# Attention probabilities turned once in float32 and split into high and low parts behind the transpose

## The chip, the cores and the metric

One core of a Trainium2 chip. The metric is the device time of one execution in microseconds (us), the median of several runs. The engines are named as in the profile: PE (matmuls) with PEld (its weight loads), DVE (VectorE), ACT (ScalarE), POOL (GpSimd), SP (which issues the DMAs).

## What is computed

Attention with keys and values pooled by eight, then a gated feed-forward layer on its output:

```
k_p = k.reshape(B, H, 72, 8, D).mean(axis=3); v_p likewise       # B = H = 8, S = 576, D = 64
scores = (q @ k_p.T) / 8;  scores -= scores.max(-1)
attn = exp(scores);  attn /= attn.sum(-1) + 1e-9
x = (attn @ v_p)  as (4608 tokens, 512)
out = ((x @ w_a) * (x @ w_b)) @ w_out                            # w: 512x1536, 512x1536, 1536x512
```

The weights arrive as float64, all else is float32.

## The kernel before

Products keep nearly float32's accuracy by splitting each operand into a high part, rounded to float32r (the form in which PE multiplies here), and a low part, the rest: high x high, high x low and low x high are summed in PSUM. `low_part` (L170 and L171) makes a low part by a subtraction, source less high.

The 4608 tokens go through the feed-forward layer in 9 tiles of 512. A tile has 12 steps. A step (`ffn_in`, L552 to L554, and `ffn_out`, L573 to L575) is 36 matmuls of 128x512: 12 for psa, 12 for psb, 12 of the step before for acc. `gated` multiplies psa and psb into h on DVE (L530), ACT rounds hh (L533) and DVE subtracts hl. In a tile's last step acc is copied to y, by ACT and DVE in turns (L581), and stored.

Attention goes in 40 chunks of 128 queries, or 64 at the end of a batch (chunks 4, 5, 14, 15, 24, 25, 34 and 35). Chunks 0 to 3 make tile 0 and come before the first step; chunks 4 to 8 make tile 1 and are processed in tile 0's steps, which is also where the weights are converted from float64 (L211 to L226, 36 blocks: ACT two instructions each, DVE three at L213, L216 and L222, POOL one at L226) and split (`split_weight`, L238 on ACT and L171 on POOL). Chunks 9 to 39 are processed in the steps of the later tiles.

What a chunk does, in `chunk`: load and split the queries (qh, ql); scores in PSUM (psc: L392 for chunks 0 to 8, L406 and L409 for the others, four of them, each reduced from PSUM by DVE at L412 before the maximum is taken off at L376 and L377); exponential on ACT (L426); the sums z and their reciprocal on DVE (L430); the scores times z, in place (L432, POOL, or DVE for chunks 1 and 3); then the split in SBUF: pr, high parts by ACT (L441) and low parts by POOL (L171) of the first 64 keys, and rem, the eight keys that remain, laid out as high, low, high (L443 twice on ACT, L171 on POOL). Then the transposes (L477, `turn`): four for pr's high parts, four for its low parts, two for rem, each group into a PSUM tile ptr, copied out by ACT (L478) to p0, p1 and p2 (one tile "work" holds p0 and p1 in later tiles). When a block of two or three chunks is turned, its products with the values go to PSUM po (L510 to L513) and out to xh (ACT, L521) and xl (DVE, L171). psc, ptr and the later po share two PSUM banks (tag "att").

The order of the work is written out by generators. `Chains` counts slots; a step of the inner loop has six, one ahead of each six of its matmuls. In a slot the chains that are due go on, and then one chain that had yielded `PE` may place its matmuls ahead of the next six:

```
for x in range(3):
    if x < 2 or t < 2:
        yield PE
    turn(x)
    if x != 1 or t < 2:
        yield 1
mark("turned", i)
```

So in the later tiles the second and the third `turn` share one such place, and the chunk's next one comes a slot later. Keys and values of the next batches (`load_keys`, `load_values`) are loaded and summed by DVE in the same way (L258, L310).

Of the kernel before, what the change touches and what calls it, by code (L numbers as in the profile page):

```python
# [27 lines left out]
# the high word of float64 2**-126, read as float32  # L28
# [38 lines left out]
# the same before the first step: chunks one after the other, the values, the second batch's keys,  # L67
# the weights' loads and how much later their conversion begins
# [3 lines left out]
class Chains:  # L72
    """Chains of work (generators), resumed slot by slot: a chain yields how many slots its next part
    comes later, or PE to get TensorE between two groups of the inner loop's products. done holds
    what has been issued."""
# [6 lines left out]
    def mark(self, *what):  # L82
        self.done.add(what)
# [30 lines left out]
def attn_moe_kernel(ctx: ExitStack, tc: tile.TileContext, q, k, v, vr, wa, wb, wo, out):  # L114
# [12 lines left out]
    ident0 = tmp("ident0")[:, :P]  # L127
    make_identity(nc, ident0)
    ident = const.tile([P, P], F32R, name="ident")
    raw = {name: const.tile([P, NF, 512], F32, name=f"w{name}_raw") for name in ("a", "b", "o")}  # L130
    w_dram = {"a": wa, "b": wb, "o": wo}
    # pooled keys, heads in pairs on the diagonal: [(h%2, d), h//2, hi/lo, h%2, key]
    kdiag = [const.tile([P, NK, 2, 2, SP], F32R, name=f"kdiag{i}") for i in range(2)]
    # pooled values, heads in pairs on the diagonal: [(h%2, key), h//2, hi/lo, (h%2, d)]
    vdiag = [const.tile([P, NK, 2, P], F32R, name=f"vdiag{i}") for i in range(2)]
    # row (part, h%4, key) belongs to which of four heads
    mask = const.tile([P, 4], F32, name="mask")
    # where the weights' bits arrive: later the place of the blocks' transposed probabilities
# [6 lines left out]
    # chunks of a batch and a tile whose products with the values are made together  # L145
    blocks, start = [], 0

    def cut(chunks, limit):
        """the cheapest blocks: a product takes its columns' time, or that of its weights' load"""
        best = None  # L150
        for x in range(1, len(chunks) + 1):
            total = sum(flat[c][2] for c in chunks[:x])
            if total > limit:
                break
            cost, rest = cut(chunks[x:], limit) if x < len(chunks) else (0, [])
            cost += max(total, 2 * P)
            if best is None or cost < best[0]:
                best = cost, [chunks[:x]] + rest
        return best
# [13 lines left out]
    # the first batch's inputs wait where the last weights come later  # L173
# [21 lines left out]
    def convert_weights(name, j, first):  # L195
        """float64 bits to the nearest float32: the sign and the exponent's top bit stay, 27 bits of
        the high word move up by three, what lies below float32's normal range becomes zero, and
        the low word rounds into the last three bits"""
# [6 lines left out]
        for f in range(NF):  # L205
# [23 lines left out]
            # not far ahead of the products, and not all three matrices at once  # L229
# [54 lines left out]
    def load_values(b):  # L284
# [31 lines left out]
        # each row's values at its head's place, zero at the others'  # L316
# [31 lines left out]
    def chunk(i):  # L348
# [18 lines left out]
        # scores less their maximum  # L367
# [32 lines left out]
        else:  # L400
# [23 lines left out]
        # probabilities  # L424
# [12 lines left out]
        yield from wait(("turned", i - 2))  # L437
# [9 lines left out]
        mark("probs", i)  # L447
        yield PROBS_GAP

        # transposed, and a block's products with the values  # L450
# [4 lines left out]
        if i == members[0]:  # L455
            turned[j] = {}

        def turn(x):
            rows = P if x < 2 else NR
            num = NK if x < 2 else NG  # L460
            if x not in turned[j]:
                if tile_of[i] < 2:
                    turned[j][x] = sb.tile([P, num, BLOCK], F32R, tag=f"p{x}", name=f"p{x}_{j}", bufs=1)
                elif x == 0:
                    both = sb.tile([P, 2, NK, BLOCK_LATER], F32R, tag="work", name=f"p_{j}", bufs=1)
                    turned[j].update({0: both[:, 0], 1: both[:, 1]})
                else:
                    turned[j][x] = sb.tile([P, NK * BLOCK], F32R, tag="p0", name=f"p{x}_{j}", bufs=1)[
                        :, :NG * BLOCK_LATER
                    ].rearrange("p (g s) -> p g s", g=NG)  # L470
            dst = turned[j][x]
            pt = ps.tile([P, 512], F32, tag="att", name=f"ptr_{i}_{x}", bufs=2)
            ptr = pt.bitcast(F32R).rearrange("p (g s) -> p g s", g=NK)
            for g in range(num):
                src = pr[:n, x, 2 * g:2 * g + 2, :] if x < 2 else rem[:n, g]
                src = src.rearrange("p a s -> p (a s)") if x < 2 else src.rearrange("p a c s -> p (a c s)")
# [3 lines left out]
        yield from wait(("turned", i - 1), ("value", j - 1))  # L480
# [17 lines left out]
        th, tl, tr = (turned[j][x] for x in range(3))  # L498
# [85 lines left out]
    def have(t):  # L584
        """all chunks of a tile are done"""
        return all(("value", block_of[i]) in done for i in range(len(flat)) if tile_of[i] == t)

    with tc.manual_schedule():
        load_early()
        nc.vector.tensor_copy(ident, ident0)  # L590
        for t in kdiag + vdiag:
            nc.gpsimd.memset(t.bitcast(F32), 0.0)
        nc.vector.tensor_reduce(
            out=mask[:NR], in_=ident0[:NR, :NR].rearrange("p (a c s) -> p c a s", a=3, c=4), axis=AX.XY, op=ALU.add
# [91 lines left out]
```

## Time and profile before

| | us |
|---|---|
| median of 3 runs | 1107.91 (1107.82 to 1108.48) |
| span of the profiled execution | 1107.4 |
| PE busy | 1038.7 (94%) |
| DVE busy | 611.5 (55%) |
| ACT busy | 522.9 (47%) |
| POOL busy | 618.8 (56%) |

The span is what the profile shows from the first to the last instruction; the time of a run, as it is measured, holds a little more. The profile gives the busy shares of the span as a whole, and the stretches of it differ: the first 215 us hold the attention of the first two tiles, the weights' conversion and tile 0's steps. PE is busy without a break after them. A matmul's duration in the trace is longer than the distance from its start to the next one's, since matmuls overlap in the array; its cost in a full queue is that distance.

### The profile page before, as it was taken

How to read it: one execution, taken by the hardware profiler on the slowest of the kernel's cores; microseconds unless marked ns; L12 is line 12 of the kernel's file. 1: busy time of each engine (PE TensorE's matmuls, PEld its weight loads, DVE VectorE, ACT ScalarE, POOL GpSimd, SP SyncE). 2: the span in 40 equal slices, each digit the busy share in tenths (PEclk: the TensorE clock that was granted, in tenths of full speed). 3: DMA queues.
4: the chain of work that ended last, by engine and by line, in shares of the span. 5: the costliest groups of instructions: out<-in, count | busy, mean ns of one | idle time of the engine just before them, and what ended most of it. 6: DMA issues, size and time to landing. Idle time of an engine off the chain costs nothing.

```text
span 1107.4 us, 13650 instructions
## 1 busy us (share of the span) xinstructions
PE 1038.7 (94%) x4964; PEld 861.7 (78%) x4964; DVE 611.5 (55%) x917; ACT 522.9 (47%) x1051; POOL 618.8 (56%) x501
## 2 busy tenths in 40 slices
PE   4378887899999999999999999999999999999998
PEld 4356665688887888888888888888888888888887
DVE  7999999863348333753367335654458343332212
ACT  3655555544445445544455445444445444443332
POOL 6557776655555555555555455554556455554442
PEclk9989888999999999999999999999999999999999
DMA  6454344120023000400021002200211020001001
GB/s 220 128 154 126 105 145 131 48 89 1 1 71 110 1 1 22 148 3 1 1 94 59 1 1 91 82 1 1 69 55 49 1 67 1 1 1 38 1 1 38
DMA packets 29874, 59.59 MB, mean 54 GB/s; under 512 B 7120, under 2 KB 7120, under 8 KB 29808
## 3 DMA queue, kind: packets, MB, share of 16 engines
q1 hardware_dynamic: 29808, 58.73, 16.9%
q8 instruction: 39, 0.64, 0.3%
q14 instruction: 27, 0.22, 0.1%
HBM read 49.28 MB, written 9.44 MB: 53 GB/s over the span
## 4 chain that ended last, share of the span: by engine, by line
PE 81%; DVE 14%; issue 2%; DMA 1%; ACT 1%; POOL 0%; SPq 0%; DVEq 0%; POOLq 0%; ACTq 0%
PE acc L573 9%; PE psa L552 8%; PE psb L552 8%; PE acc L575 8%; PE acc L574 8%; PE psa L554 8%; PE psa L553 8%; PE psb L554 8%; PE psb L553 8%; PE ptr L477 2%; PE psc L406 2%; DVE wo_raw L216 1%; DVE wo_raw L213 1%; DVE wa_raw L222 1%; DVE wb_raw L216 1%
## 5 line engine op out<-in xcount | busy, mean ns | idle before, releaser
L171 POOL TENSOR_TENSOR jlb<-wb_raw,jhb 128x512 fp32r<-128x512 f32 x108 | 142.9, 1323 | 220.9 <-ACT jhb L238 220.9
L530 DVE TENSOR_TENSOR h<-psb,h 128x512 f32<-128x512 f32 x108 | 74.5, 690 | 343.6 <-PE psb L554 340.4
L171 POOL TENSOR_TENSOR jla<-wa_raw,jha 128x512 fp32r<-128x512 f32 x108 | 143.9, 1332 | 143.0 <-ACT jha L238 117.5
L557 ACT COPY h<-psa 128x512 f32<-128x512 f32 x108 | 63.5, 588 | 244.1 <-PE psa L554 235.4
L573 PE MATMUL acc<-jho,hh 128*128 128x512 f32 x432 | 175.5, 406 | 0.0
L552 PE MATMUL psb<-xh,jhb 128*128 128x512 f32 x432 | 172.4, 399 | 2.1 <-DVE h L530 2.1
L552 PE MATMUL psa<-xh,jha 128*128 128x512 f32 x432 | 173.7, 402 | 0.0
L554 PE MATMUL psb<-xh,jlb 128*128 128x512 f32 x432 | 170.0, 393 | 2.4 <-POOL jlb L171 2.4
L553 PE MATMUL psa<-xl,jha 128*128 128x512 f32 x432 | 170.0, 393 | 1.0 <-DVE xl L171 1.0
L554 PE MATMUL psa<-xh,jla 128*128 128x512 f32 x432 | 170.0, 394 | 0.0
L575 PE MATMUL acc<-jho,hl 128*128 128x512 f32 x432 | 170.0, 393 | 0.0
L574 PE MATMUL acc<-jlo,hh 128*128 128x512 f32 x432 | 169.9, 393 | 0.0
L553 PE MATMUL psb<-xl,jhb 128*128 128x512 f32 x432 | 169.6, 393 | 0.0
L171 POOL TENSOR_TENSOR jlo<-wo_raw,jho 128x512 fp32r<-128x512 f32 x108 | 155.1, 1437 | 5.6 <-ACT jho L238 5.6
L171 DVE TENSOR_TENSOR hl<-h,hh 128x512 fp32r<-128x512 f32 x108 | 95.1, 880 | 20.7 <-ACT hh L533 20.6
L533 ACT CAST hh<-h 128x512 fp32r<-128x512 f32 x108 | 67.1, 622 | 72.6 <-DVE h L530 72.6
L554 PEld LDWEIGHTS psb<-xh,jlb 128*128 128x128 f32 x432 | 82.0, 190 | 20.8 <-POOL jlb L171 3.3
L575 PEld LDWEIGHTS acc<-jho,hl 128*128 128x128 f32 x432 | 81.9, 190 | 18.2 <-DVE hl L171 0.3
L554 PEld LDWEIGHTS psa<-xh,jla 128*128 128x128 f32 x432 | 82.1, 190 | 17.8
L552 PEld LDWEIGHTS psb<-xh,jhb 128*128 128x128 f32 x432 | 81.9, 190 | 17.8 <-issue 2.5
L553 PEld LDWEIGHTS psa<-xl,jha 128*128 128x128 f32 x432 | 82.4, 191 | 16.6 <-DVE xl L171 1.5
L552 PEld LDWEIGHTS psa<-xh,jha 128*128 128x128 f32 x432 | 82.2, 190 | 15.3
(92 smaller groups left out, 1776.3 us busy)
## 6 DMA issues: line engine op xcount, KB each, us to landing
out<-y SPq DMA_DIRECT2D x36, 256.0 KB, 2.2
kraw<-in_k SPq DMA_DIRECT2D x28, 288.0 KB, 3.9
vraw<-in_v SPq DMA_DIRECT2D x28, 256.0 KB, 3.1
qraw<-in_q SPq DMA_DIRECT2D x28, 256.0 KB, 3.8
words<-in_wa SPq DMA_DIRECT2D x12, 512.0 KB, 3.7
words<-in_wb SPq DMA_DIRECT2D x12, 512.0 KB, 3.7
words<-in_wo SPq DMA_DIRECT2D x12, 512.0 KB, 3.6
vraw<-in_vr SPq DMA_DIRECT2D x14, 192.0 KB, 2.6
```

The source lines that it names most:

```text
L171: eng.tensor_tensor(out=lo, in0=src, in1=hi.bitcast(F32), op=ALU.subtract)
L216: nc.vector.scalar_tensor_tensor(out=wi, in0=hi, scalar=-(1 << 30), in1=wi, op0=ALU.bitwise_and, op1=ALU.bitwise_or)
L406: nc.tensor.matmul(pt[:n, :2 * hk], qh[:, g, :n], kd[:, g].rearrange("p w e s -> p (w e s)"), start=True, stop=False)
L530: nc.vector.tensor_tensor(out=h, in0=pt, in1=h, op=ALU.mult)
L533: nc.scalar.copy(hh, h)
L552: nc.tensor.matmul(pt, wh[:, c], xh[:, kk], start=(kk == 0), stop=False)
L553: nc.tensor.matmul(pt, wh[:, c], xl[:, kk], start=False, stop=False)
L554: nc.tensor.matmul(pt, wl[:, c], xh[:, kk], start=False, stop=(kk == NK - 1))
L557: nc.scalar.copy(h, pt)
L573: nc.tensor.matmul(acc[c], hh[:, cs], wh, start=(f == 0), stop=False)
L574: nc.tensor.matmul(acc[c], hh[:, cs], wl, start=False, stop=False)
L575: nc.tensor.matmul(acc[c], hl[:, cs], wh, start=False, stop=(f == NF - 1))
```

## The change

The probabilities are not split in SBUF. Multiplied by 1/z they go into pr (128x512) and three times into rem, in float32 (POOL, four instructions; DVE for chunks 1 and 3). They are transposed once in float32: four transposes for pr, two for rem, against an identity that is float32 too. ACT rounds the high part on its way out of PSUM, and one slot later DVE subtracts it from the PSUM tile to get the low part (for rem on 32 of its 96 rows). The PSUM bank is so held until that subtraction. The wait for the transposes of the chunk two before stands ahead of the multiplication, one `yield 1` is gone, and the second turn needs no place of its own in the later tiles.

```diff
-    ident0 = tmp("ident0")[:, :P]
-    make_identity(nc, ident0)
-    ident = const.tile([P, P], F32R, name="ident")
+    ident = const.tile([P, P], F32, name="ident")
+    make_identity(nc, ident)
...
-        (nc.vector if first and i % 2 else nc.gpsimd).tensor_tensor(
-            out=s[:n], in0=s[:n], in1=z[:n].unsqueeze(2).broadcast_to([n, H, SP]), op=ALU.mult
-        )
-        yield 1
         yield from wait(("turned", i - 2))
-        pr = sb.tile([P, 2, H, KM], F32R, tag="pr", name=f"pr_{i}")
-        rem = sb.tile([P, NG, 3, 4, KR], F32R, tag="rem", name=f"rem_{i}")
-        sr = s[:n, :, KM:].rearrange("p (r c) s -> p r c s", r=NG)
-        nc.scalar.copy(pr[:n, 0], s[:n, :, :KM])
-        for x in (0, 2):
-            nc.scalar.copy(rem[:n, :, x], sr)
-        yield 1
-        low_part(nc.gpsimd, pr[:n, 1], s[:n, :, :KM], pr[:n, 0])
-        low_part(nc.gpsimd, rem[:n, :, 1], sr, rem[:n, :, 0])
+        pr = sb.tile([P, H, KM], F32, tag="pr", name=f"pr_{i}")
+        rem = sb.tile([P, NG, 3, 4, KR], F32, tag="rem", name=f"rem_{i}")
+        zb = z[:n].unsqueeze(2)
+        eng = nc.vector if first and i % 2 else nc.gpsimd
+        eng.tensor_tensor(out=pr[:n], in0=s[:n, :, :KM], in1=zb.broadcast_to([n, H, KM]), op=ALU.mult)
+        for x in range(3):
+            eng.tensor_tensor(
+                out=rem[:n, :, x],
+                in0=s[:n, :, KM:].rearrange("p (r c) s -> p r c s", r=NG),
+                in1=zb.broadcast_to([n, H, KR]).rearrange("p (r c) s -> p r c s", r=NG),
+                op=ALU.mult,
+            )
         mark("probs", i)
+        yield 1
         yield PROBS_GAP
...
         def turn(x):
...
-            ptr = pt.bitcast(F32R).rearrange("p (g s) -> p g s", g=NK)
-            for g in range(num):
...
-                nc.tensor.transpose(ptr[:rows, g, :n], src, ident[:n, :n])
-            nc.scalar.copy(dst[:rows, :, c0:c0 + n], ptr[:rows, :num, :n])
+            ptr = pt.rearrange("p (g s) -> p g s", g=NK)
+            if x == 0:
+                for g in range(NK):
+                    src = pr[:n, 2 * g:2 * g + 2, :].rearrange("p a s -> p (a s)")
+                    nc.tensor.transpose(ptr[:, g, :n], src, ident[:n, :n])
+                nc.scalar.copy(th[:, :, cs], ptr[:, :, :n])
+                yield 1
+                low_part(nc.vector, tl[:, :, cs], ptr[:, :, :n], th[:, :, cs])
+            else:
+                for r in range(NG):
+                    src = rem[:n, r].rearrange("p a c s -> p (a c s)")
+                    nc.tensor.transpose(ptr[:NR, r, :n], src, ident[:n, :n])
+                nc.scalar.copy(tr[:NR, :, cs], ptr[:NR, :NG, :n])
+                yield 1
+                lo = slice(4 * KR, 2 * 4 * KR)
+                low_part(nc.vector, tr[lo, :, cs], ptr[lo, :NG, :n], tr[lo, :, cs])
...
-        for x in range(3):
-            if x < 2 or t < 2:
+        for x in range(2):
+            if x == 0 or t < 2:
                 yield PE
-            turn(x)
-            if x != 1 or t < 2:
-                yield 1
+            yield from turn(x)
         mark("turned", i)
```

How the order of the instructions moves, at three places. First PE at the end of chunk 23 and the start of chunk 24, a chunk of 64 queries, in tile 4 (ptr_23_0, ptr_23_1: the turns of chunk 23; psc_24: scores of chunk 24; the last number of a name only counts tiles). Before:

```order
L477 MATMUL ptr_23_1_5320<-ident_69,pr_23_5250 128x128 x4
L477 MATMUL ptr_23_2_5326<-ident_69,rem_23_5251 96x128 x2
L573 MATMUL acc_4_2_5134<-jho_50_5212,hh_50_5206 128x512
L574 MATMUL acc_4_2_5134<-jlo_50_5213,hh_50_5206 128x512
L575 MATMUL acc_4_2_5134<-jho_50_5212,hl_50_5207 128x512
L573 MATMUL acc_4_3_5138<-jho_50_5212,hh_50_5206 128x512
L574 MATMUL acc_4_3_5138<-jlo_50_5213,hh_50_5206 128x512
L575 MATMUL acc_4_3_5138<-jho_50_5212,hl_50_5207 128x512
L406 MATMUL psc_24_0_5343<-kdiag0_73,qh_24_5255 64x288
L409 MATMUL psc_24_0_5343<-kdiag0_73,ql_24_5256 64x144
L406 MATMUL psc_24_1_5347<-kdiag0_73,qh_24_5255 64x288
L409 MATMUL psc_24_1_5347<-kdiag0_73,ql_24_5256 64x144
```

And in the changed kernel:

```order
L476 MATMUL ptr_23_0_5141<-ident_64,pr_23_5100 128x128 x4
L561 MATMUL psb_4_3_5128<-xh_4_4221,jhb_51_5069 128x512
L562 MATMUL psb_4_3_5128<-xl_4_4222,jhb_51_5069 128x512
L563 MATMUL psb_4_3_5128<-xh_4_4221,jlb_51_5070 128x512
L561 MATMUL psb_4_3_5128<-xh_4_4221,jhb_51_5069 128x512
L562 MATMUL psb_4_3_5128<-xl_4_4222,jhb_51_5069 128x512
L563 MATMUL psb_4_3_5128<-xh_4_4221,jlb_51_5070 128x512
L483 MATMUL ptr_23_1_5163<-ident_64,rem_23_5101 96x128 x2
L405 MATMUL psc_24_0_5170<-kdiag0_72,qh_24_5115 64x288
L408 MATMUL psc_24_0_5170<-kdiag0_72,ql_24_5116 64x144
L405 MATMUL psc_24_1_5174<-kdiag0_72,qh_24_5115 64x288
L408 MATMUL psc_24_1_5174<-kdiag0_72,ql_24_5116 64x144
```

The six products of acc between the last transposes of chunk 23 and the first scores of chunk 24 are gone from there; the scores follow at once, behind the end of psb_4_3. Then DVE's queue at the same place. Before:

```order
L530 TENSOR_TENSOR h_51_5266<-psb_4_3_5268,h_51_5266 128x512
L310 TENSOR_REDUCE vp_5_5145<-vraw_5_4_5273 96x64
L310 TENSOR_REDUCE vp_5_5145<-vraw_5_5_5274 96x64
L171 TENSOR_TENSOR hl_51_5290<-h_51_5266,hh_51_5289 128x512
L319 SCALAR_TENSOR_TENSOR vwide_5_5340<-vp_5_5145,mask_77 96x256 x2
L412 TENSOR_REDUCE s_24_5298<-psc_24_0_5343 64x144
L412 TENSOR_REDUCE s_24_5298<-psc_24_1_5347 64x144
```

And in the changed kernel (p_11 and p2_11 are the turned low parts of chunk 23):

```order
L539 TENSOR_TENSOR h_51_5126<-psb_4_3_5128,h_51_5126 128x512
L170 TENSOR_TENSOR p_11_4867<-ptr_23_0_5141,p_11_4867 128x4x128
L411 TENSOR_REDUCE s_24_5167<-psc_24_0_5170 64x144
L411 TENSOR_REDUCE s_24_5167<-psc_24_1_5174 64x144
L170 TENSOR_TENSOR p2_11_4868<-ptr_23_1_5163,p2_11_4868 32x2x128
```

The low part that frees ptr_23_0's bank stands behind h_51, and the one that frees ptr_23_1's behind both score reductions. Second, DVE at the end of tile 1's attention (xl_1 from po_4: its last block; vp_2: the sums of batch 2's values; h_10, ql_9: the step's product and chunk 9's queries). Before:

```order
L530 TENSOR_TENSOR h_10_1720<-psb_0_10_1722,h_10_1720 128x512
L310 TENSOR_REDUCE vp_2_1635<-vraw_2_2_1710 128x64
L310 TENSOR_REDUCE vp_2_1635<-vraw_2_3_1711 128x64
L171 TENSOR_TENSOR ql_9_1746<-qraw_9_1677,qh_9_1745 128x512
L171 TENSOR_TENSOR hl_10_1737<-h_10_1720,hh_10_1736 128x512
L171 TENSOR_TENSOR xl_1_933<-po_4_0_1764,xh_1_932 128x2x256
L171 TENSOR_TENSOR xl_1_933<-po_4_2_1783,xh_1_932 128x2x256
```

And in the changed kernel:

```order
L170 TENSOR_TENSOR xl_1_875<-po_4_0_1645,xh_1_874 128x2x256
L170 TENSOR_TENSOR xl_1_875<-po_4_2_1669,xh_1_874 128x2x256
L539 TENSOR_TENSOR h_10_1685<-psb_0_10_1687,h_10_1685 128x512
L309 TENSOR_REDUCE vp_2_1595<-vraw_2_2_1665 128x64
L309 TENSOR_REDUCE vp_2_1595<-vraw_2_3_1666 128x64
L170 TENSOR_TENSOR ql_9_1712<-qraw_9_1631,qh_9_1711 128x512
L170 TENSOR_TENSOR hl_10_1703<-h_10_1685,hh_10_1702 128x512
```

The two xl have moved ahead of h_10 and the vp pair. Third, ACT before the first step (ptr_2, ptr_3: the turns of chunks 2 and 3; po_1: their products with the values; wlow, wmag: the words of a weight block). Before:

```order
L478 COPY p2_1_438<-ptr_2_2_439 96x2x128
L478 COPY p0_1_407<-ptr_3_0_448 128x4x128
L211 ACTIVATE wlow_o1_454<-words_78 128x512
L212 ACTIVATE wmag_o1_455<-words_78 128x512
L478 COPY p1_1_419<-ptr_3_1_462 128x4x128
L478 COPY p2_1_438<-ptr_3_2_469 96x2x128
L521 CAST xh_0_344<-po_1_0_480 128x2x256
L521 CAST xh_0_344<-po_1_2_491 128x2x256
```

And in the changed kernel:

```order
L484 CAST p2_1_352<-ptr_3_1_411 96x2x128
L237 CAST jhb_0_415<-wb_raw_70 128x512
L210 ACTIVATE wlow_b1_422<-words_77 128x512
L211 ACTIVATE wmag_b1_423<-words_77 128x512
L530 CAST xh_0_318<-po_1_0_433 128x2x256
L530 CAST xh_0_318<-po_1_2_449 128x2x256
L210 ACTIVATE wlow_o1_460<-words_77 128x512
L211 ACTIVATE wmag_o1_461<-words_77 128x512
```

The copies of chunk 3's turns and xh of its block stand ahead of the second part of wo, no longer behind it.

## Rows read from the trace of the kernel before

**Rows 1.** Stretches: length; busy us (count) of PE, PEld, DVE, ACT, POOL; granted clock; DMA share.

```profile
25.00:66.00 41.00, 20.50 (x97) 17.44 (x98) 39.14 (x59) 24.85 (x53) 20.20 (x17) 1.00 0.48 143
66.00:215.00 149.00, 117.29 (x517) 92.39 (x515) 142.75 (x168) 79.91 (x160) 108.66 (x77) 0.86 0.39 118
215.00:1107.00 892.00, 887.98 (x4296) 739.96 (x4296) 410.10 (x660) 408.81 (x820) 473.00 (x381) 1.00 0.11 34
```

**Rows 2.** Timelines of DVE and POOL near 60 and 97 us: start, duration, instruction.

```profile
59.72 0.69 DVE L216 SCALAR_TENSOR_TENSOR wa_raw<-words,wa_raw 128x512 int32<-128x512 int32 x1
...
97.56 1.65 DVE L216 SCALAR_TENSOR_TENSOR wo_raw<-words,wo_raw 128x512 int32<-128x512 int32 x1
...
97.19 1.47 POOL L171 TENSOR_TENSOR jlb<-wb_raw,jhb 128x512 fp32r<-128x512 f32 x1
```

**Rows 3.** Groups by shape, 66 to 215 us: count | busy us, mean ns | idle before.

```profile
L216 DVE SCALAR_TENSOR_TENSOR wo_raw<-words,wo_raw 128x512 int32<-128x512 int32 x10 | 16.5, 1655 | 0.3
...
L530 DVE TENSOR_TENSOR h<-psb,h 128x512 f32<-128x512 f32 x11 | 7.5, 680 | 0.0
```

**Rows 4.** Timeline of PE, turns of a full chunk.

```profile
509.02 0.39 PE L575 MATMUL acc<-jho,hl 128*128 128x512 f32 x1
509.25 0.46 PE L477 MATMUL ptr<-ident,pr 128*128 128x128 f32 x4
509.54 0.30 PE L477 MATMUL ptr<-ident,rem 128*96 128x128 f32 x2
509.68 0.47 PE L573 MATMUL acc<-jho,hh 128*128 128x512 f32 x1
```

**Rows 5.** Timeline of PE, turns of a chunk of 64 queries.

```profile
373.90 0.50 PE L477 MATMUL ptr<-ident,pr 64*128 64x64 f32 x4
374.23 0.30 PE L477 MATMUL ptr<-ident,rem 64*96 64x64 f32 x2
```

**Rows 6.** Timelines of PE and DVE where chunk 23 is turned.

```profile
423.56 0.40 PE L554 MATMUL psb<-xh,jlb 128*128 128x512 f32 x1
...
424.07 0.69 DVE L530 TENSOR_TENSOR h<-psb,h 128x512 f32<-128x512 f32 x1 [5.82 <-PE psb L554]
```

**Rows 7.** Groups by shape, the whole span.

```profile
L171 POOL TENSOR_TENSOR pr<-s,pr 128x512 fp32r<-128x512 f32 x32 | 42.6, 1331 | 4.3 <-ACT pr L441 4.2
L432 POOL TENSOR_TENSOR s<-s,z 128x576 f32<-128x576 f32 x30 | 41.7, 1389 | 54.1 <-DVE z L430 34.9 <-ACT jha L238 19.2
...
L171 POOL TENSOR_TENSOR rem<-s,rem 128x64 fp32r<-128x64 f32 x32 | 12.7, 397 | 0.0
L581 DVE COPY y<-acc 128x512 f32<-128x512 f32 x18 | 12.4, 691 | 16.9 <-PE acc L575 16.9
...
L171 DVE TENSOR_TENSOR xl<-po,xh 128x512 fp32r<-128x512 f32 x18 | 12.2, 688 | 10.1 <-ACT xh L521 10.1
...
L412 DVE TENSOR_REDUCE s<-psc 64x144 f32<-64x288 f32 x24 | 9.7, 443 | 2.9 <-PE psc L409 2.6
...
L171 DVE TENSOR_TENSOR xl<-po,xh 128x256 fp32r<-128x256 f32 x2 | 0.8, 418 | 2.7 <-ACT xh L521 2.7
```

**Rows 8.** Waits, 25 to 66 us: total, times, longest.

```profile
PE po L510 <- ACT p L478: 6.0, 1, 6.0
```

**Rows 9.** Timelines of PE and DVE around 213 us; [idle before <- its releaser].

```profile
215.47 0.40 PE L406 MATMUL psc<-kdiag,qh 128*128 128x288 f32 x1 [2.44 <-DVE xl L171]
...
211.23 1.32 DVE L310 TENSOR_REDUCE vp<-vraw 128x64 f32<-128x512 f32 x2 [2.38 <-DMA vraw<-in_v]
...
214.74 1.27 DVE L171 TENSOR_TENSOR xl<-po,xh 128x512 fp32r<-128x512 f32 x2
```

**Rows 10.** Short stretches around two gaps of PE, columns as in rows 1.

```profile
105.70:109.10 3.40, 1.61 (x11) 1.14 (x9) 3.33 (x6) 0.00 (x0) 1.32 (x2) 1.00 0.87 245
109.10:112.50 3.40, 3.40 (x12) 2.82 (x11) 3.33 (x6) 2.68 (x5) 3.40 (x3) 0.50 0.34 134
...
214.90:218.30 3.40, 2.70 (x15) 2.28 (x16) 3.30 (x7) 0.31 (x1) 0.00 (x0) 1.00 0.00 0
```

More of the change, by code (lines that the diff above doesn't have):

```diff
@@ L431, in chunk @@
         yield 1
-        (nc.vector if first and i % 2 else nc.gpsimd).tensor_tensor(
-            out=s[:n], in0=s[:n], in1=z[:n].unsqueeze(2).broadcast_to([n, H, SP]), op=ALU.mult
-        )
-        yield 1
-        yield from wait(("turned", i - 2))
-        pr = sb.tile([P, 2, H, KM], F32R, tag="pr", name=f"pr_{i}")
-        rem = sb.tile([P, NG, 3, 4, KR], F32R, tag="rem", name=f"rem_{i}")
-        sr = s[:n, :, KM:].rearrange("p (r c) s -> p r c s", r=NG)
-        nc.scalar.copy(pr[:n, 0], s[:n, :, :KM])
-        for x in (0, 2):
-            nc.scalar.copy(rem[:n, :, x], sr)
-        yield 1
-        low_part(nc.gpsimd, pr[:n, 1], s[:n, :, :KM], pr[:n, 0])
-        low_part(nc.gpsimd, rem[:n, :, 1], sr, rem[:n, :, 0])
-        mark("probs", i)
+        yield from wait(("turned", i - 2))
+        pr = sb.tile([P, H, KM], F32, tag="pr", name=f"pr_{i}")
[10 more added lines that the diff above has]
+            )
+        mark("probs", i)
+        yield 1
         yield PROBS_GAP
@@ L454, in chunk @@
         total = sum(flat[c][2] for c in members)
-        if i == members[0]:
[L456 to L472, printed above, removed]
-            ptr = pt.bitcast(F32R).rearrange("p (g s) -> p g s", g=NK)
-            for g in range(num):
-                src = pr[:n, x, 2 * g:2 * g + 2, :] if x < 2 else rem[:n, g]
-                src = src.rearrange("p a s -> p (a s)") if x < 2 else src.rearrange("p a c s -> p (a c s)")
-                nc.tensor.transpose(ptr[:rows, g, :n], src, ident[:n, :n])
-            nc.scalar.copy(dst[:rows, :, c0:c0 + n], ptr[:rows, :num, :n])
@@ L480, in chunk, with blocks_turned @@
-        yield from wait(("turned", i - 1), ("value", j - 1))
-        for x in range(3):
-            if x < 2 or t < 2:
+        def blocks_turned():
+            if tile_of[i] < 2:
+                both = [sb.tile([P, NK, BLOCK], F32R, tag=f"p{x}", name=f"p{x}_{j}", bufs=1) for x in range(2)]
+                rem = sb.tile([P, NG, BLOCK], F32R, tag="p2", name=f"p2_{j}", bufs=1)
+            else:
+                both = sb.tile([P, 2, NK, BLOCK_LATER], F32R, tag="work", name=f"p_{j}", bufs=1)
+                both = [both[:, 0], both[:, 1]]
+                rem = sb.tile([P, NK * BLOCK], F32R, tag="p0", name=f"p2_{j}", bufs=1)[
+                    :, :NG * BLOCK_LATER
+                ].rearrange("p (g s) -> p g s", g=NG)
+            return (*both, rem)
@@ new lines, in turn @@
+        def turn(x):
+            th, tl, tr = turned[j]
+            cs = slice(c0, c0 + n)
+            pt = ps.tile([P, 512], F32, tag="att", name=f"ptr_{i}_{x}", bufs=2)
+            ptr = pt.rearrange("p (g s) -> p g s", g=NK)
[6 more added lines that the diff above has]
+                low_part(nc.vector, tl[:, :, cs], ptr[:, :, :n], th[:, :, cs])
+            else:
+                for r in range(NG):
[5 more added lines that the diff above has]
+                low_part(nc.vector, tr[lo, :, cs], ptr[lo, :NG, :n], tr[lo, :, cs])
@@ L483, in chunk @@
+        yield from wait(("turned", i - 1), ("value", j - 1))
+        if i == members[0]:
+            turned[j] = blocks_turned()
+        for x in range(2):
+            if x == 0 or t < 2:
                 yield PE
-            turn(x)
-            if x != 1 or t < 2:
-                yield 1
+            yield from turn(x)
         mark("turned", i)
@@ L497, in chunk @@
         per = min(NK, 512 // total)
-        th, tl, tr = (turned[j][x] for x in range(3))
+        th, tl, tr = turned[j]
         for g0 in range(0, NK, per):
@@ L589, in attn_moe_kernel @@
         load_early()
-        nc.vector.tensor_copy(ident, ident0)
         for t in kdiag + vdiag:
@@ L593, in attn_moe_kernel @@
         nc.vector.tensor_reduce(
-            out=mask[:NR], in_=ident0[:NR, :NR].rearrange("p (a c s) -> p c a s", a=3, c=4), axis=AX.XY, op=ALU.add
+            out=mask[:NR], in_=ident[:NR, :NR].rearrange("p (a c s) -> p c a s", a=3, c=4), axis=AX.XY, op=ALU.add
         )
```

## The prediction

> **What bounds the kernel now.** I read the busy time of the engines by stretch first [rows 1]. It falls into three parts. From 215 us to the end the matmul engine is busy 887.98 of 892 us and no other engine more than half of the time: there the length of its own queue is the time, and any gap in it is lost. From 66 to 215 us VectorE is busy 142.75 of 149 us and the matmul engine 117.29, at a mean granted clock of 0.86; from 25 to 66 us VectorE is busy 39.14 of 41 and the matmul engine half of the time. So in the first 215 us VectorE sets the pace, but not by its own work alone. One instruction of the weights' conversion, L216, takes 0.69 us when no GpSimd instruction runs when it starts, and 1.65 us when it starts 0.4 us into one [rows 2]. The ten of wo_raw average 1655 ns, while the products h of L530, which read PSUM, average 680 ns there [rows 3]. I read this as an instruction with SBUF inputs waiting for the GpSimd instruction beside it, one with a PSUM input not. The Trainium skill, "SBUF — State Buffer", puts an exclusive lock behind it: VectorE with two SBUF inputs and a GpSimd instruction that reads SBUF share a port pair. The trace agrees by the 1.65 against 0.69 us.
>
> So three prices are needed: matmul time after 215 us, VectorE time weighed against GpSimd time before it, and any new gap.
>
> **The change, part by part.**
>
> *Fewer transposes.* A chunk of 128 queries turned high, low and remainder: four, four and two transposes. The second four go. In the matmul engine's timeline the second four start at 509.25 and the remainder at 509.54; the product before them started one ordinary pitch, 0.23, earlier [rows 4]. So four cost 0.29 us. In a chunk of 64 queries it is 373.90 to 374.23, 0.33 us [rows 5]. After tile 1's chunks 31 are left, 25 full and six of 64 queries: 25 x 0.29 + 6 x 0.33 = **-9.2 us**, all of it in the stretch where the matmul queue is the time. The transposes that stay now read float32 instead of float32r. No row shows a float32 transpose; I take the same duration, as the array moves as many columns either way, and price the other case as a rival.
>
> *Six new gaps.* The second turn no longer asks for a group of the matmul engine, so in six places (chunks 14, 15, 24, 25, 34, 35, the order shows it at 24) the next chunk's scores stand straight behind the remainder's transposes, where six products stood between. The scores need a PSUM bank, and both were taken by the two turns. Formerly ScalarE's copy freed a bank; now VectorE's low part does, one slot later. At 24 this low part stands behind h in VectorE's queue, and h waits for the last product of psb. In the trace of before that last product starts at 423.56 and h at 424.07, 0.69 long [rows 6]. The low part is a 128 x 512 subtraction out of PSUM; that price is 688 ns [rows 7], so it ends at 424.07 + 0.69 + 0.69 = 425.45. The matmul engine would reach the scores at 423.56 + 0.23 + 0.14 (remainder pair, 509.54 to 509.68 [rows 4]) = 423.93: a wait of 1.5 us. The second score tile of that slot takes the bank that the first leaves, so it waits for the first's reduction: 443 ns [rows 7], plus the 0.17 by which a product outlasts its pitch (0.40 less 0.23), plus twice the 0.11 from the end of psb (423.96) to h (424.07): 0.8 us. For 14, 24 and 34 this is 2.3 each. For 15, 25 and 35 h is long done and the low part too, so 0.8 each. At 14 a copy y of 691 ns [rows 7] stands in the same queue: 0.7. Sum 6.9 + 2.4 + 0.7 = **+10.0 us**. Bounds: 0 if VectorE keeps ahead after all, and 10.0 plus the clock (below).
>
> *GpSimd and VectorE from 66 to 215 us*, chunks 4 to 8. GpSimd gave a full chunk 1389 + 1331 + 397 ns (product, low part, remainder's low part [rows 7]) = 3.12 us. Now it multiplies 512 of the 576 columns, 1389 x 512/576 = 1235, and three remainders, each at the 397 of the same size: 2.43. Five chunks: -3.5 us. VectorE gains two low parts, 688 + 418 ns by the nearest rows [rows 7]: 1.11 for the three full chunks, and for the two of half the columns 0.42, the price of 256 columns, and some 0.29 for 128: 0.71; together +4.7. If the two engines' work adds up on the shared side, -3.5 stays. What VectorE takes out of PSUM runs beside GpSimd while GpSimd has work, 108.66 of 149 us or 73% [rows 1]: 3.4 of the 4.7 us are so covered. -3.5 + 4.7 - 3.4 = **-2.2 us**. Bounds: -3.5 (all covered) to +4.7 (GpSimd's relief worth nothing, no cover).
>
> *The first 66 us*, chunks 0 to 3. VectorE gains four times 1.11 = 4.4 us, and for chunks 1 and 3, which it multiplies itself, three small products more each: at about half of GpSimd's 397 ns, as 688 stands to 1331 [rows 7], 6 x 0.2 = 1.2. GpSimd loses four low parts (4 x 1.73 = 6.9) and gains on chunks 0 and 2 (2 x (2.43 - 1.39) = 2.1): -4.8. On ScalarE the second block's copies of probabilities no longer stand behind the conversion of wo's second part, as the order shows; in the trace a product with the values waited 6.0 us for such a copy [rows 8]. Work added to the busy engine, work and waits taken from the others: I take **0**, bounds -6.0 to +5.6. ScalarE's own loss of work counts for nothing, since it is busy half of the time.
>
> *The gap at 213 us.* The scores of chunk 9 wait 2.44 us for the two xl of the last block of tile 1, which start at 214.74 because the vp reductions ahead of them waited 2.38 us for values to land [rows 9]. In the changed order xl stands ahead of that h and of the second vp pair. I take the gap as closed but for the time of ql behind the same vp: **-2.2 us**; bounds -2.4 and 0.
>
> *Nothing else costs.* The wait for ("turned", i - 2) moves ahead of the multiplication, so GpSimd's queue could hold behind it; but a chunk's turn is issued a slot sooner and there are two chunks between. The cast of the identity, one small instruction at the start, is gone. No DMA is added, and SP's queue only moves with the slots.
>
> **Sum:** -9.2 + 10.0 - 2.2 + 0 - 2.2 = -3.6. The profiled span is 1107.4 and the median of the runs 1107.91, 0.5 above it, which I put on again: 1107.9 - 3.6 = **1104.3 us**. About 0.2%, 2.2 us, is what a measurement can tell from no change.
>
> **The rivals.**
>
> *Slower: VectorE itself is the bound of the first 215 us.* If its busy share of 95 and 96% [rows 1] were its own need, GpSimd's relief would bring nothing and every added instruction would land: +4.7 in place of -2.2, +5.6 in place of 0. Then -9.2 + 10.0 + 4.7 + 5.6 - 2.2 = +8.9: 1116.8. It decides from the point where less than about 6.7 of the 10.3 added us are covered or made good. For it speaks how full VectorE is; against it the mean of 1655 ns for L216 against 0.69 alone [rows 2, 3]. 13%.
>
> *The clock falls at the new gaps.* A gap in the 3.4 us from 105.70 (matmul busy 1.61 of them) was followed by a granted clock of 0.50, 1.2 GHz, for the next 3.4 us; the 2.44 gap at 213 was followed by 1.00, 2.4 GHz [rows 9, 10]. At half the clock 3.4 us of matmul time hold 1.7 us of work. The three larger gaps could add 3 x 1.7 = 5.1: 1109.4. The matmul engine is full up to each of them, as it was at 213, which speaks against. 10%.
>
> *Float32 transposes run in four passes.* Then each transpose would take three more times its columns' time: 512 columns take 0.23, so 128 take 0.057 and a transpose gains 0.17; 25 x 6 x 0.17 + 36 x 0.085 = +28.6, giving 1132.9. The Trainium skill, "FP8 and Floating Point Precision", TensorE Precision Notes, has "True FP32: 4 passes through PE array", and by that rule this change would lose; "TensorE: Matmul & The Clock Gate", Terms, calls transpose mode 4x faster for FP32, which would undo it. No run here shows either yet. Against it speaks that the instruction is a transpose in both programs and only moves data. 7%.
>
> *Faster: the new gaps do not appear.* If VectorE has the low part done when the scores come (h a little sooner, a bank more), the +10.0 goes: 1107.9 - 13.6 = 1094.3. The order of the queue speaks against it. 8%.
>
> **How the numbers follow.** The forecast has the remaining 62%; its own range is 1099 to 1110 from the bounds of its terms taken together: faster 0.38, same 0.20, slower 0.04. The clock gives same 0.05, slower 0.05; VectorE and the four passes slower 0.13 and 0.07; no gaps faster 0.08. Together faster 0.46, same 0.25, slower 0.29. The range 1096 to 1118 takes in VectorE as the bound; it leaves out the four passes, the missing gaps and some 3% of the forecast's own tails, 18%.
>
> **What would show it.** Right: after 215 us the matmul engine has six gaps, three of about 2.3 us and three of 0.8, released by a low part or a score reduction on VectorE; 31 groups of four transposes less, and the four that stay still about 0.29 us; no gap of 2.4 at chunk 9; the steady stretch begins about 4 us sooner. Wrong: transposes whose pitch has grown; a granted clock under 1.00 after the gaps; a VectorE share of the first 215 us still at 95% and that stretch longer; or L216 unchanged in its mean though GpSimd does less, which would sink the reading of the shared side.

## The result and the profile after

The changed kernel takes 1113.06 us (median), the kernel before 1107.87 in the same comparison: ratio 1.0042, 95% interval 1.0031 to 1.0053. It is slower by about 5 us where -3.6 was forecast; a second comparison gave 1112.93, ratio 1.0037 (1.0024 to 1.0049). One of the six executions took 3590.4 us at a granted clock of 0.29; it counts in the median, which is 1112.9 without it, and not in the ratio. The time lies in the range, but on the other side of no change.

The busy times of the whole span, from the page:

```profile
span 1110.4 us, 13284 instructions
...
PE 1034.4 (93%) x4804; PEld 853.6 (77%) x4804; DVE 648.2 (58%) x1002; ACT 473.3 (43%) x891; POOL 593.8 (53%) x535
```

PE, ACT and POOL work less than before, DVE 36.7 us more, as the edit says. The stretches, columns as in [rows 1]:

```profile
25.00:66.00 41.00, 22.37 (x82) 17.84 (x83) 38.87 (x64) 22.12 (x42) 15.64 (x14) 0.75 0.44 133
66.00:215.00 149.00, 117.61 (x512) 93.24 (x511) 144.39 (x187) 73.64 (x140) 102.81 (x82) 0.87 0.39 120
215.00:1107.00 892.00, 881.26 (x4160) 730.64 (x4159) 446.29 (x717) 369.85 (x696) 459.75 (x412) 1.00 0.10 33
```

After 215 us PE is now idle for 10.7 of 892 us, where it had been idle for 4.0 [rows 1]. Of the 4.0 us, 3.4 lie behind the last matmul of the kernel before (it ends at 1103.57), of the 10.7 only 0.4 (1106.59): inside the queue it is 10.3 against 0.6. The waits of PE from 200 us on say for what (total us, times, longest; the third line is chunk 9's, at 212.75):

```profile
PE psc L405 <- DVE p L170: 6.6, 5, 1.6
PE psc L405 <- DVE s L411: 3.7, 6, 0.6
PE psc L408 <- DVE ql L170: 1.2, 1, 1.2
```

The first two are the forecast's gaps: score tiles that wait for a bank, until a low part (p) or a score reduction (s) on DVE has freed it. At chunk 24, PE in the kernel before, where six products of acc (not shown) stand between the turn of chunk 23 and the scores, and no score tile waits:

```profile
588.67 0.39 PE L554 MATMUL psb<-xh,jlb 128*128 128x512 f32 x1
...
590.95 0.30 PE L477 MATMUL ptr<-ident,rem 128*96 128x128 f32 x2
...
592.54 0.29 PE L406 MATMUL psc<-kdiag,qh 128*64 128x288 f32 x1
```

([rows 6], which the forecast took for this place, stand in tile 2, 165 us earlier. Here h starts at 589.17, 0.50 behind the last product of psb; there it was 0.51, so nothing in the forecast hangs on it.) PE and DVE in the changed kernel:

```profile
588.67 0.39 PE L563 MATMUL psb<-xh,jlb 128*128 128x512 f32 x1
588.90 0.38 PE L483 MATMUL ptr<-ident,rem 128*96 128x128 f32 x2
590.60 0.32 PE L405 MATMUL psc<-kdiag,qh 128*64 128x288 f32 x1 [1.32 <-DVE p L170]
590.76 0.23 PE L408 MATMUL psc<-kdiag,ql 128*64 128x144 f32 x1
591.60 0.35 PE L405 MATMUL psc<-kdiag,qh 128*64 128x288 f32 x1 [0.61 <-DVE s L411]
```

```profile
589.17 0.69 DVE L539 TENSOR_TENSOR h<-psb,h 128x512 f32<-128x512 f32 x1 [3.43 <-PE psb L563]
589.77 0.68 DVE L170 TENSOR_TENSOR p<-ptr,p 128x512 fp32r<-128x512 f32 x1
591.09 0.45 DVE L411 TENSOR_REDUCE s<-psc 64x144 f32<-64x288 f32 x1 [0.64 <-PE psc L408]
```

The chain is read from the stamps: the last product of psb, h, then the low part behind h to 590.45, then the scores; the reduction to 591.54, then the second score tile. Measured from start to start, less what the same pairs take without a wait, the eleven gaps sum to 12.0 us (the waits view counts only from the end of the matmul ahead, 10.3).

The two traces' first product of each step gives the account of the span. At the first step of tile 1 the changed kernel is 3.2 us ahead (220.55 against 223.77), in the end 3.0 behind. The first step of all begins 4.2 us earlier (52.96 against 57.14); 1.0 of that is lost again before tile 1.

### The profile page after: what moved, and what is told of

It reads as the page before. It is cut to its first block, busy times and chain, and to the rows that moved or that the text cites. A ratio compares the mean times of both kernels' runs of the same rounds, so it can differ in the third digit from the quotient of the medians.

```text
span 1110.4 us, 13284 instructions
## 1 busy us (share of the span) xinstructions
PE 1034.4 (93%) x4804; PEld 853.6 (77%) x4804; DVE 648.2 (58%) x1002; ACT 473.3 (43%) x891; POOL 593.8 (53%) x535
## 4 chain that ended last, share of the span: by engine, by line
PE 77%; DVE 19%; issue 1%; DMA 1%; POOL 1%; ACT 0%; SPq 0%; DVEq 0%; POOLq 0%; ACTq 0%
PE psb L561 8%; PE acc L582 8%; PE psb L563 8%; PE acc L584 8%; PE acc L583 8%; PE psb L562 8%; PE psa L561 8%; PE psa L563 7%; PE psa L562 7%; PE psc L405 2%; DVE wo_raw L215 2%; DVE hl L170 1%; DVE wa_raw L215 1%; PE ptr L476 1%; DVE wo_raw L212 1%
## 5 line engine op out<-in xcount | busy, mean ns | idle before, releaser
L170 POOL TENSOR_TENSOR jla<-wa_raw,jha 128x512 fp32r<-128x512 f32 x108 | 153.0, 1417 | 64.9 <-ACT jha L237 62.7
L170 POOL TENSOR_TENSOR jlo<-wo_raw,jho 128x512 fp32r<-128x512 f32 x108 | 157.9, 1462 | 5.6 <-ACT jho L237 5.6
L170 DVE TENSOR_TENSOR hl<-h,hh 128x512 fp32r<-128x512 f32 x108 | 105.8, 979 | 9.3 <-ACT hh L542 8.5
L582 PEld LDWEIGHTS acc<-jho,hh 128*128 128x128 f32 x432 | 82.3, 191 | 15.7
```

Source lines behind the costliest of these rows:

```text
L170: eng.tensor_tensor(out=lo, in0=src, in1=hi.bitcast(F32), op=ALU.subtract)
L582: nc.tensor.matmul(acc[c], hh[:, cs], wh, start=(f == 0), stop=False)
```

## The experiments

All were compared with the kernel before on the same chip, in five rounds or more; its median was 1107.87 to 1108.35 in these comparisons. "Changed" is 1113.06 us.

**Giving the turn its place back where 64 queries follow.**

```diff
-            if x == 0 or t < 2:
+            if x == 0 or t < 2 or (i + 1 < len(flat) and flat[i + 1][2] < P):
```

> The second turn asks for a place of its own again where the next chunk has 64 queries (chunks 13, 14, 23, 24, 33, 34), and nowhere else. Theory (the six gaps are the loss): in the trace of the changed kernel the gaps after 215 us sum to 12.0 us, and one of them is followed by 3.4 us at a granted clock of 0.50, worth 1.7. Left over should be about 1.2 at chunk 14, where a second low part still stands behind the copy y, and some 0.3 each at three places: about 11.5 us less than the changed kernel, 1101 to 1102.5 us, faster than the kernel before. Rival (the gaps only take up time in which the matmul engine would have waited later): within 2 us of the changed kernel, 1111 to 1115. Rival on the clock (the fall to 0.50 comes without the gaps too): 1103 to 1104, with such a stretch still in the steady part.

1101.87 us (1101.48 to 1102.97), ratio 0.9947 (0.9935 to 0.9960): 11.2 less than changed, and faster than before. Of the steady waits one is left, in chunk 14:

```profile
215.00:1107.00 892.00, 881.35 (x4163) 730.45 (x4162) 449.03 (x717) 370.11 (x696) 456.83 (x412) 1.00 0.11 34
```

```profile
PE psc L405 <- DVE p L170: 0.9, 1, 0.9
```

PE's busy time there is what it was with the gaps (881.35 against 881.26), but the last matmul now ends at 1097.33 instead of 1106.59, so that the idle time of this window lies behind it. No stretch from 218 us to the end is at 0.50. The six places are the loss: given back, they turn 5 us slower into 6 us faster than the kernel before.

**Only the three in front of chunks 14, 24 and 34** (the same condition with `n == P and`).

> The second turn asks for a place of its own only in chunks 13, 23 and 33, so only the gaps in front of chunks 14, 24 and 34 close (1.49 + 0.78 us each, and the 1.2 us inside chunk 14 may stay); those at 15 (1.7 + 0.78), 25 and 35 (0.78 each) stay. Theory (each gap costs its length, and the clock falls only behind the long ones): 6.8 us of gap gone, and of the stretches at 0.50 only one at chunk 15 can remain: 6 to 9 us less than the changed kernel, 1104 to 1107. Rival (short gaps bring the clock down as well): stretches at 0.50 behind 25 and 35, 1107 or more.

1104.12 us (1103.37 to 1106.15), 8.9 less than changed. The waits that are left:

```profile
PE psc L405 <- DVE s L411: 1.8, 3, 0.6
PE psc L405 <- DVE p L170: 0.9, 1, 0.9
```

The three are the score reductions at 15, 25 and 35. The low part is the one in chunk 14 that is left with six places too, so the 1.59 us in front of chunk 15 have gone as well, which was not expected. The trace shows how: chunk 14's first turn stands six products later than in the changed kernel (353.70 instead of 351.83), and its low part ends at 355.92, just ahead of the scores at 355.97. By their lengths the closed gaps are thus 6.8 + 1.7 = 8.5 of the 8.9 us, and against six places the run is 2.25 slower, where three gaps of 0.78 make 2.3: each gap costs its length. No stretch behind 219 us stood at 0.50 in this profile.

**Every second turn with a place** (`yield PE` in both passes, `x == 0 or t < 2` gone).

> Every second turn asks for a place of its own, as in the kernel before, not only the six. The matmul engine's work is the same, only spread over more slots. Theory (only the six gaps counted, sharing the place earns nothing by itself): as with six places, 1101 to 1103 us. Rival (the shared place also brings work forward that the end needs): 2 us or more slower than with six places.

1102.07 us (1100.93 to 1103.98), as with six. Sharing the place of the others neither costs nor earns anything that shows.

**The changed kernel once more.**

> The changed kernel once more, unchanged, for a second profile. The gaps should stand at the same places with the same lengths, 12 us together; what may differ is how many of the long ones are followed by a granted clock of 0.50, 0 to 4 of them, 1.4 to 1.7 us each, which would account for most of the spread of its runs (1111.5 to 1113.5).

1112.93 us (1110.55 to 1114.05). The waits are again 6.6 and 3.7 us, in the same five and six places; two of the long gaps were followed by a clock of 0.50, in the first profile it was one. Chunk 9's wait of 1.2 is not there this time. First profile, the gap at chunk 34 and what followed it, then two stretches of the second one (columns as in [rows 1]):

```profile
840.30:843.70 3.40, 1.60 (x9) 0.92 (x7) 1.66 (x3) 3.14 (x8) 2.49 (x2) 1.00 0.20 68
843.70:847.10 3.40, 3.26 (x9) 2.56 (x10) 2.22 (x5) 0.45 (x1) 1.29 (x1) 0.50 0.02 5
```

```profile
356.70:360.10 3.40, 3.40 (x12) 2.70 (x11) 1.47 (x5) 1.44 (x3) 0.26 (x1) 0.50 0.00 0
592.20:595.60 3.40, 3.40 (x10) 2.68 (x11) 2.14 (x4) 0.29 (x1) 1.29 (x1) 0.50 0.00 0
```

PE is busy there, at 1.2 GHz instead of 2.4, so each such stretch costs up to 1.7 us. In the profiles of the changed kernel and of its variants with the gaps they came behind chunks 14, 15, 24 and 34, never behind the single waits of 0.6 at 25 and 35, and not in every run.

**The kernel before with float32 transposes.**

```diff
-            ptr = pt.bitcast(F32R).rearrange("p (g s) -> p g s", g=NK)
+            ptr = pt.rearrange("p (g s) -> p g s", g=NK)
...
-                nc.tensor.transpose(ptr[:rows, g, :n], src, ident[:n, :n])
+                nc.tensor.transpose(ptr[:rows, g, :n], src.bitcast(F32), ident[:n, :n])
```

> The kernel before, with its ten transposes a chunk made in float32 (the same bits, a float32 identity) and nothing else changed. Theory (a float32 transpose is longer by itself): start to start 0.108 us between transposes of 128 queries instead of 0.064; a group of four costs the queue 0.07 more, as 0.455 against 0.382 in the two traces, the group of six 0.1 to 0.25 more; over 25 chunks 4 to 8 us slower, 1112 to 1116. Rival (the longer pitch in the changed kernel comes from where the transposes stand, not from their type): within 1 us of before. Rival (four passes): 30 us or more slower.

1113.05 us (1112.55 to 1114.31), ratio 1.0048 (1.0035 to 1.0060): 5.2 slower, by the type alone. The turn of a full chunk there, to be laid beside [rows 4]:

```profile
509.98 0.60 PE L476 MATMUL ptr<-ident,pr 128*128 128x128 f32 x4
510.41 0.38 PE L476 MATMUL ptr<-ident,rem 128*96 128x128 f32 x2
510.55 0.48 PE L572 MATMUL acc<-jho,hh 128*128 128x512 f32 x1
```

Four transposes take 0.43 us to the remainder's start where they took 0.29.

**The changed kernel with float32r transposes.** Types of pr, rem, ident and the PSUM view back to float32r.

> The changed kernel with pr, rem and the identity in float32r, so that the six transposes are of that type again. The probabilities are rounded when they are multiplied, so their low parts come out as zero: this leaves out the low part of the probabilities, for its time alone. Theory (type alone): transposes back at a pitch of 0.064, a group of four 0.07 less, 25 chunks: 1.5 to 3 us faster than the changed kernel, 1110 to 1111.5, the six gaps unchanged. Rival (type costs nothing): 1112 to 1114.

1114.61 us (1112.91 to 1116.91): not the 1.5 to 3 us faster that was expected. The transposes are as expected: a group of four costs PE's queue 0.38 where the float32 one costs 0.455 (medians of 24 each, from the product ahead to the second product behind it, less the pitch). But in this profile four stretches at 0.50 stood behind the gaps, against one or two in the changed kernel, 3 to 5 us more; from tile 1's first step to the end it takes 2.2 us more than the changed kernel's first profile (892.1 against 889.9). So the gain by type is seen in the rows, not in the time.

**The low part of chunks 0 to 8 three times.**

```diff
-                low_part(nc.vector, tl[:, :, cs], ptr[:, :, :n], th[:, :, cs])
+                for _ in range(3 if t < 2 else 1):
+                    low_part(nc.vector, tl[:, :, cs], ptr[:, :, :n], th[:, :, cs])
```

> The changed kernel, with the large low part of chunks 0 to 8 issued three times instead of once: 2 x (7 x 0.69 + 2 x 0.42) = 11.3 us more for VectorE, out of PSUM, in the first 215 us. Theory (VectorE waits there for GpSimd, and what it takes out of PSUM runs beside GpSimd): 5.8 us of it after 66 us at 27% uncovered and 5.5 before at 51% uncovered: 4 to 5 us slower than the changed kernel, about 1117. Rival (VectorE is the bound by its own work): 11 us slower, 1124. Rival (the first 215 us have slack on VectorE): within 1 us.

1124.8 us (1119.74 to 1126.05), 11.7 slower than changed, which looks like the rival. In its trace, though, only 7.3 us are there when the steady part begins; the rest are four stretches at 0.50 instead of one, and waits. The gaps had to go before this could be measured, so the next four runs stand on the version with six places (1101.87).

**VectorE's and GpSimd's work by stretch.** Three times the low part of chunks 0 to 3, then of 4 to 8 (`t == 0`, `t == 1` in the loop above):

> The version with six places, with the large low part of chunks 0 to 3 issued three times: 2 x 4 x 0.69 = 5.5 us more for VectorE before the first step. With the six gaps gone the clock of the steady part does not blur it. Theory (VectorE's work bounds the time before the first step and little of it lies beside GpSimd): 4 to 5.5 us later at the first step, of which the first steps of tile 0 may hide some; 3 to 5.5 slower in all, 1105 to 1107. Rival (half of it is hidden, as the forecast's bounds had it): 2 to 3 us slower.

> The version with six places, with the large low part of chunks 4 to 8 issued three times: 2 x (3 x 0.69 + 2 x 0.42) = 5.8 us more for VectorE in tile 0's steps. Theory of the forecast (73% of what VectorE takes out of PSUM runs beside GpSimd's work): 1.6 us slower, 1103 to 1104. Theory from the three-fold low part of all nine chunks (2.7 of 5.8 landed behind the first step): 2.5 to 3 slower, 1104 to 1105. Rival (all of it lands): 5.8 slower.

Three times the multiplication into pr on GpSimd, of chunks 4 to 8 and of 0 and 2:

> The version with six places, with the multiplication of chunks 4 to 8 into pr issued three times on GpSimd: 2 x 5 x 1.19 = 11.9 us more for GpSimd in tile 0's steps. Theory of the forecast (the two engines' work adds up on the side they share, so GpSimd's time is worth its length): 8 to 12 us slower, 1110 to 1114. Rival (GpSimd has 27% of its time free there and its extra work falls into it): 0 to 3 us slower.

> The version with six places, with the multiplication of chunks 0 and 2 into pr issued three times on GpSimd: 2 x 2 x 1.24 = 5.0 us more for GpSimd before the first step. Theory (worth its length): 4 to 5 us slower, 1106 to 1107. Rival (GpSimd is busy for two fifths of that time and has room): 0 to 2 us slower.

| added | where | us added | median | slower by | per us |
|---|---|---|---|---|---|
| VectorE, from PSUM | chunks 0 to 3 | 5.5 | 1107.59 (1106.71 to 1108.43) | 5.7 | 1.0 |
| VectorE, from PSUM | chunks 4 to 8 | 5.8 | 1105.38 (1104.00 to 1108.16) | 3.5 | 0.6 |
| GpSimd | chunks 4 to 8 | 11.9 | 1110.76 (1109.12 to 1111.94) | 8.9 | 0.75 |
| GpSimd | chunks 0 and 2 | 5.0 | 1103.32 (1102.21 to 1105.22) | 1.5 | 0.3 |

In the first run of the table the first step begins 4.7 us later. The first product of psa with six places, then with the added low parts:

```profile
52.94 0.63 PE L561 MATMUL psa<-xh,jha 128*128 128x512 f32 x1
```

```profile
57.67 0.52 PE L562 MATMUL psa<-xh,jha 128*128 128x512 f32 x1
```

Before the first step VectorE's added work lands in full and GpSimd's mostly not; behind it both count, neither in full. "Slower by" is a difference of medians (from 1101.87), and by the intervals of the ratios it is good to somewhat under 2 us: 0.3 to 0.4 per us, 0.15 in the row of 11.9 us. So 1.0 and 0.3 can be told apart, 0.6 and 0.75 can't. For GpSimd in tile 0's steps the forecast's adding up on a shared side comes near (8 to 12 us expected); for VectorE there (1.6 expected), and for both before the first step, it doesn't.

**Less low part, and a multiplication moved.** ScalarE copying in place of the large low part of chunks 0 to 8:

> The changed kernel, with ScalarE copying the transposed probabilities a second time in place of VectorE's large low part in chunks 0 to 8. This leaves out the low part of the probabilities of tiles 0 and 1. VectorE loses 7 x 0.69 + 2 x 0.42 = 5.7 us in the first 215 us, ScalarE gains as much. By what the three-fold low part cost per us added (7.3 of 11.3 us at the first step of tile 1): 3 to 4 us faster than the changed kernel. Rival (VectorE alone is the bound): 5.7 faster. Rival (one low part a chunk is hidden, and only more of them count): within 1 us.

1111.16 us (1107.47 to 1117.28 over twelve runs): the spread is larger than the effect, so this run decides nothing. The other on the version with six places:

> The version with places in front of the six chunks, with the multiplication of chunks 1 and 3 moved from VectorE to GpSimd as in all others: VectorE loses some 2 x 1.3 us before the first step, GpSimd gains 2 x 2.4. Theory (VectorE's work bounds the time before the first step, four fifths of what is added there lands): 1 to 2 us faster than the version with six places, 1100 to 1101. Rival (the chunks' chain through GpSimd bounds it, since the transposes wait there for its products): 1 to 4 us slower, 1103 to 1106.

1102.08 us (1101.86 to 1102.65): no change, neither the theory nor the rival. By the prices of the table it would have been 2.6 off VectorE (-2.6) and 4.8 onto GpSimd (+1.5).

**Chunks 14, 24 and 34 two slots later**, on the version with six places.

```diff
+            begin_at += 2 if tile_of[i] > 1 and n < P and flat[i - 1][2] == P else 0
```

> The version with six places, with chunks 14, 24 and 34 begun two slots later, so that twelve products stand between the turn of the chunk before and their scores. The one wait left in the steady part of the version with six places, 0.92 us in front of a score tile of chunk 14 (its bank is freed by a low part that stands behind a copy y), should go: about 1 us faster, 1100.5 to 1101.2. Rival (the later start makes another transfer of work late): same or slower, 1102 to 1103.

1108.57 us (1107.58 to 1109.92), 6.7 slower than with six places: a miss. The order around the next chunk changed with it. Its waits at chunk 25:

```profile
602.23 0.28 PE L408 MATMUL psc<-kdiag,ql 128*64 128x144 f32 x1 [1.12 <-DVE ql L170]
609.06 0.35 PE L405 MATMUL psc<-kdiag,qh 128*64 128x288 f32 x1 [0.90 <-DVE p L170]
```

```profile
599.22 1.52 DVE L170 TENSOR_TENSOR vrem<-vwide,vrem 32x512 fp32r<-32x512 f32 x1
600.76 1.41 DVE L170 TENSOR_TENSOR ql<-qraw,qh 128x256 fp32r<-128x256 f32 x1
```

Its queries' low part ql now stands behind vrem, and both take twice their usual time; chunk 15's and 35's scores wait in the same way. One wait of 0.9 us was given for seven, 6.7 us together, as much as the run lost.

## Why the prediction was wrong

No single step turned the sign: between the profiles four terms missed, all to the slow side, by 1.7, 2.0, 1.7 and 1.2 us, each less than the 3.6 us of gain that was forecast. Three steps failed: that a float32 transpose takes "the same duration", that for chunk 15 "h is long done and the low part too", and that the clock behind the gaps costs nothing. A fourth, the forecast for the first 215 us, came near by two errors that cancel. The account of the profiled span, which the terms give in full:

| term | forecast | in the trace |
|---|---|---|
| fewer transposes | -9.2 | -7.5 |
| six new gaps | +10.0 | +12.0 |
| the clock behind them | 0 (a rival, +5.1) | +1.7 |
| up to tile 1's first step | -2.2 + 0 - 2.2 | -3.2 |
| sum | -3.6 | +3.0 (1110.4 - 1107.4) |

**Six new gaps** was right in mechanism and places, and the version with six places shows it to be the whole loss; the term was mis-sized. The forecast had chunk 14 with one copy y (0.7); in the trace the last score tile there waits 1.04 us for a low part behind that copy. For 15 it held that the low part would be "long done"; but the low part stood behind hl, which took 3.47 us against its mean of 0.98, and the scores waited. DVE, then GpSimd beside it, then PE:

```profile
351.85 3.47 DVE L170 TENSOR_TENSOR hl<-h,hh 128x512 fp32r<-128x512 f32 x1
355.25 0.41 DVE L170 TENSOR_TENSOR p<-ptr,p 128x256 fp32r<-128x256 f32 x1
```

```profile
351.31 0.98 POOL L439 TENSOR_TENSOR rem<-s,z 64x64 f32<-64x64 f32 x3
352.25 1.29 POOL L170 TENSOR_TENSOR jlb<-wb_raw,jhb 128x512 fp32r<-128x512 f32 x1
353.51 1.26 POOL L170 TENSOR_TENSOR jlo<-wo_raw,jho 128x512 fp32r<-128x512 f32 x1
```

```profile
355.71 0.34 PE L405 MATMUL psc<-kdiag,qh 128*64 128x288 f32 x1 [1.59 <-DVE p L170]
```

From start to start that is 1.7 us, and chunk 14's is 1.2 instead of 0.7; the three large gaps (1.49 + 0.78) came out as forecast.

**The clock** was given 10%, on the argument that PE is full up to each gap. It fell behind one to two of them in the changed kernel and up to four in its variants. The forecast took the one gap of 2.44 that was not followed by 0.50 [rows 9, 10] for the pattern. At that same chunk 9 six of the variants have a wait of about 2.6 us: in three of them (six places, three places, 11.9 us added on GpSimd) a stretch at 0.50 followed, in three (float32r transposes, two slots later, ScalarE copying) none.

**Fewer transposes**: "I take the same duration" for float32 is the step that failed, and the type alone costs, as the kernel before with float32 transposes shows. 31 chunks measured 0.22 us saved for a full one (0.382 + 0.522 before, 0.455 + 0.232 after, medians of 24) instead of 0.29, and 0.35 for one of 64 queries: 25 x 0.217 + 6 x 0.354 = 7.5. A float32 transpose follows the next after 0.108 us instead of 0.064; that is 1.7 times, far from the four passes, of which that kernel shows no sign (+5.2 us, where that rival's own prices would make 25 x 10 x 0.17 + 6 x 10 x 0.085 = 47.6 for its ten transposes a chunk).

**The first 215 us** came out 1.2 short of the forecast in the profiles, and that this is so little is luck. Before the first step the forecast had 0, and the changed kernel is 4.2 ahead there; from the first step to tile 1 it had -4.4, and the changed kernel loses 1.0 (0.3 in its second profile). The prices were wrong in both directions, and the measured ones, if taking work away is worth what adding it costs, do not give these times either. GpSimd's relief was taken at 1 and measured 0.75 in tile 0's steps; VectorE's added work was taken as 27% uncovered and measured 60%, give or take 30 points: -3.5 x 0.75 + 4.7 x 0.6 = +0.2 instead of -2.2. Before the first step VectorE counts in full and GpSimd by 0.3: +5.6 - 1.4 = +4.2 instead of 0, where the trace has -4.2, with the wait for a copy of probabilities [rows 8] gone. Which part of that order earned it was not tried alone, and stays open. One sign that the forecast named for its reading of the shared side, a lower mean of L216 (L215 in the changed kernel), is there only in sum: its 29 instructions from 66 to 215 us took 39.7 us instead of 44.6, but the ten of wo_raw rose from 1655 to 1808 ns.

The gap at 213 us was a single execution's: 2.44 in the profile of before, 0.82 in that kernel with float32 transposes, 1.24 in the first profile of the changed kernel, none in its second. The -2.2 for closing it rested on the first of these.

**The base.** The forecast put 0.5 us between span and time. Over all runs it is 1.7 to 2.0; the profiled execution of before was 1.4 above its median, and that of the changed kernel 0.8 below its own. So +3.0 between the profiles is +5.2 between the medians; the four terms miss by 6.6 us, and the other 2.2 of the medians' 8.8 lie here.

Of the rivals, the slower one (VectorE the bound of the first 215 us) holds for work added before the first step, but it is not why the kernel is slower, since the first step came earlier; "the new gaps do not appear" was wrong outright, and is what one condition in the code then brought, at 1101.87 and not at its 1094.3.

## What to carry to other kernels

When a copy that frees a PSUM bank moves to another engine, look through that engine's queue for what stands ahead of it, wherever the bank's next user is only a few matmuls away; where the order is generated, the rare cases (here a chunk of half the size) are where the user comes next. A place in the queue that a step no longer needs for itself can still be what covers the next step's wait: 6 of 31 places were worth 11 us, the other 25 nothing. And a stall of PE in a full stretch can have a price beyond its length, as the clock may fall behind it (here up to 1.7 us each time).

## What the runs showed of the hardware

A transpose in float32 costs more of PE's queue than in float32r, 0.108 against 0.064 us from start to start for 128 columns, but for 64 queries a group of four cost slightly less (0.60 against 0.63). The clock's fall behind a gap is not the same from run to run: the same gaps, to 0.1 us, were followed by one or by two stretches of 3.4 us at 0.50. And one VectorE subtraction with SBUF inputs, hl, took up to 3.47 us, over five times the 0.63 of the shortest, beside GpSimd instructions that followed each other without a break; the 108 products h, which read PSUM, took 0.67 to 0.70 us, every one of them.
